# Gated attention and feed-forward decode: wq and the first four key units split between two issuing engines

## The chip, the core and the metric

The kernel runs on one core of a Trainium2 chip. The core has five engines with their own instruction streams: TensorE (PE, matrix products), VectorE (DVE), ScalarE (ACT), GpSimd (POOL) and SyncE (SP). SyncE and ScalarE can each issue transfers (DMAs); the data is moved by sixteen DMA engines that all issuers share. An instruction stream runs in program order, and an engine that waits for a semaphore holds up all that stands behind the waiting instruction, the issue of transfers too. The metric is the device time of one execution in microseconds (us), as a median over runs.

## The reference

One token (`x`, 512 numbers) goes through an attention block with a long cache and through a gated feed-forward block, and a sigmoid gate mixes the two:

```python
g = sigmoid((x * gate_w).sum(-1))
q = x @ wq                                  # 32 heads of 128, wq 512 x 4096 (8 MB)
scores = q . k_cache * 128 ** -0.5          # 8 key heads, each used by 4 query heads, 32768 keys of 128
a = softmax(scores) . v_cache @ wo          # wo 4096 x 512
b = (silu(x @ w1) * (x @ w3)) @ w2          # 1792 wide
out = g * a + (1 - g) * b
```

All of it is float32. Keys and values are 128 MiB each, read once; all that is read comes to 296.23 MB.

## The kernel before, in words

**Buffers and units.** Keys and values come in units of 8 MB: 128 partitions by 16384 numbers, so a row of 64 KB in each partition. Two buffers of that size, `big[0]` (called A) and `big[1]` (B), take everything that is streamed. Each buffer has a left and a right half of 32 KB a partition, `region(b, z)` with z = 0 or 1, and the program tracks them under the keys A0, A1, B0 and B1. There are sixteen key units (t = 0 to 15, two heads to four units) and sixteen value units, which run four units behind (`LAG = 4`). `wq` goes to A first. Key units 0 and 2 go to B, units 1 and 3 to A (`where(t)`); from unit 4 on keys go to A and values to B.

**The order of the work.** Nothing is scheduled automatically. `Program` (L24) records each instruction in the order in which `add` is called, works out from the tiles read and written which semaphores it must wait for, and then each engine's list is emitted as it stands. A transfer is one more instruction in the list of the engine that issues it. `load` (L190) records a transfer on SyncE; nine semaphores ("lanes") are used in turn. So the place of a `load` call among the other calls decides where it stands in SyncE's list, and the tiles that it overwrites decide what it waits for.

**The start.** SyncE issues `wq` (L203), then key unit 0 (`load_keys(0)`, L488), neither with a wait. ScalarE issues the small transfers of `x` and `gate_w` (L202, 2 KB each). TensorE turns `x` into columns (L253), VectorE copies them to `xp` (L259), and 64 products with `wq` follow (L268), which need both `xp` and all of `wq`. ScalarE then does the gate's activation (L280), copies the query out of the accumulators (L286), and after two transposes copies it in sixteen pieces to `win` (L296). `winc` (L324) is the window on `win` that TensorE uses as weights for the scores.

**One key unit.** For unit t, ScalarE copies three quarters of the right half to a spare tile (`set_aside`, L318), VectorE transposes the keys in eight steps of 32 columns (L346; four from the left half, one from the right half, three from the spare tile), and TensorE multiplies each step with `winc` (L330). VectorE's steps alternate between two tiles, so a step waits for the products of the step before the last. Afterwards ScalarE copies the scores out of the accumulator (`scores_out`, L358), and the next unit's transfer is recorded after these (L502), before `winc` of the next unit. Every fourth unit a softmax follows (`turn`, `softmax`). After unit 3 the feed-forward weights w1 and w3 are loaded into B (L454) and multiplied (L463); from then on each round also loads and uses a value unit (L413, L432). The tail (L529 to L690) finishes the last heads and streams wo and w2 in pieces.

Of the kernel before, what the change touches and what calls it, by code (L numbers as in the profile page):

```python
# [116 lines left out]
def kernel(  # L117
# [13 lines left out]
    nc = tc.nc  # L131
# [5 lines left out]
    NC = D // P  # L137
# [7 lines left out]
    R = NB * DH  # L145
    NP = HKV // 2
    NH = 4 * NP
    LAG = 4
# [12 lines left out]
    def sbuf(name, *shape):  # L161
        return nc.alloc_sbuf_tensor(name, [P, *shape], F32)[:]

    big = [sbuf("big_a", 2 * R), sbuf("big_b", 2 * R)]
# [20 lines left out]
    ps_s, ps_o, *pm = [nc.alloc_psum_tensor(f"ps{i}", [P, 512], F32)[:] for i in range(4)]  # L185


    lanes = [0]

    def load(dst, src, writes, over=()):  # L190
        lanes[0] += 1
        lane = f"load{lanes[0] % 9}"
        return pr.add(
            "SP", lambda: nc.sync.dma_start(dst, src), writes=writes, over=[*over, lane], inc=lane, by=16, also=lane,  # L194
        )

    def region(b, z):
        return big[b][:, z * R:(z + 1) * R]


    for i, t in enumerate((x.rearrange("a b n -> (a b) n"), gate_w.rearrange("(o n) -> o n", o=1))):
        pr.add("ACT", lambda i=i, t=t: nc.scalar.dma_start(rows[i][0:1, :], t), writes=[f"row{i}"], inc="row", by=16)  # L202
    load(big[0], wq.rearrange("(p c) n -> p (c n)", c=NC), ["A0", "A1"])  # L203


    ident, ones, fold = sbuf("ident", P), sbuf("ones", P), sbuf("fold", 32)
# [37 lines left out]
    def clear(**kw):  # L244
        pe(zeros,
           reads=["acc"], writes=["s"], **kw)
# [40 lines left out]
    for b in range(2):  # L287
        qt = kt[b][:, 0:512]
        dve(lambda b=b, qt=qt: V.transpose(qt, rows[b]), reads=[f"row{b}"], writes=[f"kt{b}"])
        for j in range(4):  # L290
            w, u = divmod(4 * b + j, 2)
            src = qt[32 * j:32 * j + 32, :].rearrange("p (q c x) -> p x c q", q=4, c=4)[:, 0]
            for e in range(2):
                r, o = 2 * u + e, 16 + 8 * e + 4 * u
                dst = win[32 * r:32 * r + 32, w, :, o:o + 4]
# [5 lines left out]
    kd = k_cache.rearrange("a (w u) s d -> w (a u s d)", u=2).rearrange("w (p m r) -> w m p r", p=P, m=4)  # L301
    vd = v_cache.rearrange("a h (e p n) d -> (a h) e p (n d)", e=2, p=P)

    def where(t):
        return 1 if t in (0, 2) else 0

    def load_keys(t):
        b = where(t)
        load(big[b], kd[t // 4, t % 4], ["AB"[b] + str(z) for z in range(2)])
# [6 lines left out]
    def set_aside(t):  # L316
        src, key = region(where(t), 1).rearrange("p (n r) -> p n r", n=NB), "AB"[where(t)] + "1"
        act(lambda: A.copy(spare, src[:, :, 32:128]), reads=[key], writes=["wo"])  # L318
        if t == LAG - 1:
            act(lambda: A.copy(extra, src[:, :, 0:32]), reads=[key], writes=["extra"], over=["B1"])  # L320

    def window(t, z):
        return act(
            lambda: A.copy(winc, win[:, t // 4, :, 16 - 16 * z:48 - 16 * z]),  # L324
            reads=[("win", t // 4, r) for r in range(4)], writes=["winc"], credit="windows",
        )
# [9 lines left out]
    def scores(t, z, win_op):  # L336
        kin = region(where(t), z).rearrange("p (n c j) -> p c n j", c=4, j=32)
        ks = []
        for c in range(4):
            src, key = kin[:, c], "AB"[where(t)] + str(z)  # L340
            if (z, c) >= (1, 1):
                src, key = spare[:, :, 32 * (c - 1):32 * (c - 1) + 32], "wo"
            elif z == 1 and t == LAG - 1:
                src, key = extra, "extra"
            dst = kt[c % 2].rearrange("p (n i) -> p n i", i=32)
            k = dve(lambda d=dst, s=src: V.transpose(d, s), reads=[key], writes=[f"kt{c % 2}"], credit="keys")  # L346
            pe(lambda c=c: scores_part(c), reads=[f"kt{c % 2}", "winc"], writes=["s"], loop=True,
               credits=((win_op, 1), (k, 1)) if c == 0 else ((k, 1),))
            ks.append(k)

        if t == LAG - 1 and z == 0:
            done = dve(lambda: V.tensor_copy(mark2, ones[:, 0:1]), reads=["ones"], writes=["mark2"])
            for k in ks:
                k.via = done

    def scores_out(t):
        o = act(
            lambda: A.copy(sb[:, :, :, t % 4], ps_s.rearrange("p (n i) -> p n i", i=32)),  # L358
            reads=["s"], writes=[("sb", t % 4)], credit="scores",
        )  # L360
        return o
# [9 lines left out]
    def turn(loop, credits=()):  # L371
        for f in range(4):
            pe(lambda f=f: turn_part(f), reads=[("sb", m) for m in range(4)] + ["ident"], writes=[f"f{f}"], loop=loop,
               credits=credits if f == 0 else ())
# [29 lines left out]
    def total(w):  # L404
        dve(lambda: V.tensor_reduce(  # L405
            sums[:, 8 * w:8 * w + 8].rearrange("p (u q) -> p u q", u=2),
            probs[:, :, 0:1024].rearrange("p u (n q) -> p u q n", q=4), axis=AX.X, op=ALU.add,
        ), reads=[("prob", u) for u in range(2)], writes=[("sums", w)])


    def load_values(s):
        return pr.add(
            "SP", lambda: nc.sync.dma_start(big[1], vd[s // 2, s % 2]), writes=["B0", "B1"], over=["extra"],  # L413
            credit="values", by=16,
        )

    def weights(s):
        u, e = s // 2 % 2, s % 2
        return act(
            lambda: A.copy(  # L420
                pv[:, 0:512].rearrange("p (y r) -> p y r", r=64),
                prob[u][:, 0:1024].rearrange("p (y e r) -> p y e r", e=2, r=64)[:, :, e],
            ), reads=["pvpad", ("prob", u)], writes=["pv"], over=["o"], credit="weights",
        )
# [13 lines left out]
    def values_loop(vt, wt, credits):  # L438
        pe(values_all, reads=["B0", "B1", "pv", "pvpad"], writes=["o"], credits=(*credits, (vt, 16), (wt, 1)), loop=True)


    def own(s):
        h, e = divmod(s, 2)
        dve(lambda: V.tensor_tensor(
            tmp[:, e], ps_o.rearrange("p (b d) -> p b d", b=4), own_b.unsqueeze(2).to_broadcast([P, 4, P]), op=ALU.mult,
        ), reads=["o", "own_b"], writes=[f"tmp{e}"])
        if e == 1:
            dve(lambda: V.tensor_reduce(red[h], tmp.rearrange("p e b d -> p d (e b)"), axis=AX.X, op=ALU.add),  # L448
                reads=["tmp0", "tmp1"], writes=[("red", h)])


    def load_hidden():
        for z, t in enumerate((w1, w3)):
            load(big[1][:, z * NC * F:(z + 1) * NC * F], t.rearrange("(p c) f -> p (c f)", c=NC), [f"B{z}"])  # L454

    def hidden_products():
        for z in range(2):
            def ff(z=z):
                t = big[1][:, z * NC * F:(z + 1) * NC * F]
                for c in range(NC):  # L460
                    for j in range(4):
                        o = c * F + FJ * j
                        ins = T.matmul(  # L463
                            pm[z][32 * j:32 * j + 32, 0:FJ], xp[:, c, :], t[:, o:o + FJ],
                            start=(c == 0), stop=(c == NC - 1),
                        )
                return ins
            pe(ff, reads=[f"B{z}", "xp"], writes=[f"m{z}"])
# [16 lines left out]
        pr.add(e, lambda: q.dma_start(outs[2 * i:2 * i + 2, :], src[31 + 64 * i:33 + 64 * i, :]),  # L485
               reads=[key], writes=[("out", i)], inc=inc, by=16)

    load_keys(0)  # L488
    vals = {}
    first = window(0, 0)  # L490
    for t in range(NH):
        v = t - LAG
        set_aside(t)
        scores(t, 0, first)
        scores(t, 1, window(t, 1))
        out_op = ((scores_out(t), 1),)
        if v < 0:
            clear(loop=True, credits=out_op)
        if t == LAG - 1:
            load_hidden()  # L500
        if t + 1 < NH:
            load_keys(t + 1)  # L502
            first = window(t + 1, 0)
        if v >= 1:
            own(v - 1)
        if t % 4 == 3:
            turn(v >= 0, out_op if v >= 0 else ())
        if v >= 0:
            values_loop(vals.pop(v), weights(v), () if t % 4 == 3 else out_op)
            clear(loop=True)  # L510
        if t == LAG - 1:
            hidden_products()
        if v + 1 >= 0 and t + 1 < NH:
            vals[v + 1] = load_values(v + 1)

        if t % 4 == 3:
            softmax(t // 4)
        if t % 4 == 0 and t > 0:
            total(t // 4 - 1)
        if t == LAG:  # L520
            hidden()
# [175 lines left out]
    a, b, c, d = flips  # L697
# [67 lines left out]
```

## Time and profile before

| | |
|---|---|
| median of 3 runs | 694.2 us (694.1 to 694.31) |
| profiled execution | 693.89 us, of which the span of instructions is 692.1 us |
| moved by DMA | 296.35 MB, mean 428 GB/s |
| busy | PE 388.3 us (56%), DVE 370.1 (53%), ACT 134.7 (19%), POOL 2.8 |

In rows of the profile an instruction stands as line, engine, operation, what it writes and reads, and its shape; "x8" is a count. In the listing by time the first two numbers are start and duration in us from the start of the span, and the brackets say how long the engine was idle before and what ended that. "SPq" and "ACTq" are the parts of SyncE and ScalarE that issue transfers; the duration of such a row is that of the issue, not of the movement, and when a transfer has landed is seen at the instruction that waited for it. The engines' busy shares are averages over the whole span.

### The profile page before, as it was taken

To read this page: it belongs to the slowest core of one execution; us is meant where nothing else is said; L and a number is where in the kernel's file an instruction comes from. 1 tells how busy PE (TensorE), PEld (TensorE's weight loads), DVE (VectorE), ACT (ScalarE), POOL (GpSimd) and SP (SyncE) were. 2 spreads that over 40 slices of the span, in tenths; PEclk is the share of its full clock that TensorE was granted. 3 is DMA by queue.
4 is the path that set the end of the run, shared out by engine and by line. 5 is a ranking of instruction groups with operands and counts; after the bars stand their busy time and mean duration, and the time that the engine had idled before them with its cause. 6 is when DMAs were issued, how large, how long until landed. Compare 5 with 4: busy or idle time off the path is not lost. (4 is left out here: it accounts for less than half of the span.)

```text
span 692.1 us, 5789 instructions
## 1 busy us (share of the span) xinstructions
PE 388.3 (56%) x2448; PEld 95.3 (14%) x2448; DVE 370.1 (53%) x259; ACT 134.7 (19%) x113; POOL 2.8 (0%) x15
## 2 busy tenths in 40 slices
PE   1537677566473636565564646364563646564457
PEld 0101111201010101201010101101010101211112
DVE  1049998493725637493826537492816547600701
ACT  0143323222303131220303131220303031100000
POOL 1000000000000000000000000000000000000000
PEclk9969999968686966778695779788697879865789
DMA  9999999999999999999999999999999999999996
GB/s 394 444 432 424 428 424 432 449 439 432 424 432 424 443 447 432 428 428 428 432 443 443 428 428 428 428 443 447 432 424 428 428 436 439 421 451 425 422 429 287
DMA packets 6213, 296.35 MB, mean 428 GB/s; under 512 B 694, under 2 KB 698, under 8 KB 1084
## 3 DMA queue, kind: packets, MB, share of 16 engines
q1 hardware_dynamic: 6196, 296.23, 99.1%
q8 instruction: 6, 0.10, 0.1%
q14 instruction: 3, 0.02, 0.0%
q10 hardware_dynamic: 8, 0.01, 0.0%
HBM read 296.23 MB, written 0.00 MB: 428 GB/s over the span
## 5 line engine op out<-in xcount | busy, mean ns | idle before, releaser
L346 DVE STREAM_TRANSPOSE aside<-big_a 128x2048 f32<-128x2048 f32 x41 | 94.4, 2302 | 184.3 <-DMA big_a<-in_A_k_cache_dram 184.3
L330 PE MATMUL ps<-aside,winc 128*32 128x512 f32 x512 | 89.4, 776 | 168.0 <-PEq L703 167.2
L330 PE MATMUL ps<-kt,winc 128*32 128x512 f32 x512 | 89.0, 772 | 49.1 <-PEq L703 49.1
L318 ACT COPY aside<-big_a 128x6144 f32<-128x6144 f32 x14 | 74.4, 5313 | 171.2 <-DMA big_a<-in_A_k_cache_dram 171.2
L432 PE MATMUL ps<-big_b,pv 128*32 128x512 f32 x768 | 94.9, 650 | 17.4 <-PEq L703 17.4
L346 DVE STREAM_TRANSPOSE kt<-aside 128x2048 f32<-128x2048 f32 x32 | 72.7, 2273 | 0.0
L346 DVE STREAM_TRANSPOSE kt<-big_a 128x2048 f32<-128x2048 f32 x28 | 63.5, 2269 | 0.0
L330 PEld LDWEIGHTS ps<-aside,winc 128*32 128x32 f32 x512 | 13.1, 120 | 236.6 <-issue 236.6
L358 ACT COPY sb<-ps 128x512 f32<-128x512 f32 x16 | 17.1, 1071 | 136.5 <-PE ps L330 136.5
L432 PEld LDWEIGHTS ps<-big_b,pv 128*32 128x32 f32 x768 | 27.7, 119 | 85.0 <-issue 85.0
L346 DVE STREAM_TRANSPOSE aside<-aside 128x2048 f32<-128x2048 f32 x16 | 36.3, 2269 | 0.0
L587 PE MATMUL ps<-big_b,probs 128*32 128x512 f32 x128 | 19.1, 756 | 21.1 <-DMA big_b<-in_A_v_cache_dram 21.1
L330 PEld LDWEIGHTS ps<-kt,winc 128*32 128x32 f32 x512 | 13.1, 120 | 125.4 <-issue 125.4
L596 DVE TENSOR_SCALAR red<-ps,own_b 128x128 f32<-128x128 f32 x2 | 0.7, 350 | 52.7 <-PE ps L587 52.7
L324 ACT COPY winc<-win 128x128 f32<-128x128 f32 x32 | 9.8, 307 | 77.9 <-PE ps L330 77.9
L587 PE MATMUL ps<-big_a,probs 128*32 128x512 f32 x128 | 18.1, 730 | 7.6 <-DMA big_a<-in_A_v_cache_dram 7.6
L346 DVE STREAM_TRANSPOSE aside<-big_b 128x2048 f32<-128x2048 f32 x7 | 16.0, 2291 | 11.0 <-DMA big_b<-in_A_k_cache_dram 11.0
L641 PE MATMUL ps<-win,ones 128*128 128x512 f32 (+1 forms) x40 | 21.8, 631 | 0.0
L242 PE MATMUL ps<-acc 128*128 128x512 f32 x34 | 20.0, 670 | 2.5 <-POOL acc L213 1.5
L379 DVE TENSOR_REDUCE mt<-turned 128x8 f32<-128x2048 f32 x4 | 9.2, 2292 | 20.3 <-PE turned L368 20.3
L405 DVE TENSOR_REDUCE sums<-probs 128x8 f32<-128x2048 f32 x4 | 15.3, 3834 | 2.1 <-ACT probs L398 2.1
L268 PE MATMUL turned<-big_a,xp 128*32 128x512 f32 x64 | 8.6, 699 | 12.0 <-DMA big_a<-in_A_wq_dram 12.0
(94 smaller groups left out, 186.9 us busy)
## 6 DMA issues: line engine op xcount, KB each, us to landing
big_b<-in_A_v_cache_dram SPq DMA_DIRECT2D x2, 4096.0 KB, 25.8
big_b<-in_B_w_dram SPq DMA_DIRECT2D x2, 3584.0 KB, 20.8
aside<-in_A_wo_dram SPq DMA_DIRECT2D x1, 4096.0 KB, 29.4
big_a<-in_A_wo_dram SPq DMA_DIRECT2D x1, 4096.0 KB, 20.4
big_a<-in_B_w_dram SPq DMA_DIRECT2D x2, 1024.0 KB, 23.5
big_a<-in_B_w_dram SPq DMA_DIRECT2D x1, 768.0 KB, 26.0
big_a<-in_B_w_dram SPq DMA_DIRECT2D x1, 512.0 KB, 26.7
big_a<-in_B_w_dram SPq DMA_DIRECT2D x1, 256.0 KB, 26.9
```

The lines of the kernel that those rows point to most:

```text
L242: return T.matmul(ps_s, acc[:, 0:P], acc, start=True, stop=False, skip_group_check=True)
L268: ins = T.matmul(pf[b][32 * j:32 * j + 32, :], xp[:, c, :], t[:, o:o + REP * DH], start=(c == 0), stop=(c == NC - 1),)
L318: act(lambda: A.copy(spare, src[:, :, 32:128]), reads=[key], writes=["wo"])
L324: lambda: A.copy(winc, win[:, t // 4, :, 16 - 16 * z:48 - 16 * z]),
L330: ins = T.matmul(ps_s[32 * g:32 * g + 32, :], winc[:, c, :], kt[c % 2][:, 512 * g:512 * g + 512], start=False, stop=False, skip_group_chec ...
L346: k = dve(lambda d=dst, s=src: V.transpose(d, s), reads=[key], writes=[f"kt{c % 2}"], credit="keys")
L358: lambda: A.copy(sb[:, :, :, t % 4], ps_s.rearrange("p (n i) -> p n i", i=32)),
L379: dve(lambda: V.tensor_reduce(mt[:, 0:8], turned.rearrange("p (n q) -> p q n", q=8), axis=AX.X, op=ALU.max), reads=banks, writes=["mt"])
L405: dve(lambda: V.tensor_reduce(sums[:, 8 * w:8 * w + 8].rearrange("p (u q) -> p u q", u=2), probs[:, :, 0:1024].rearrange("p u (n q) -> p u ...
L432: ins = T.matmul(ps_o[32 * t:32 * t + 32, :], pv[:, o:o + 32], big[1][:, n * P:(n + 4) * P], start=((z, g) == (0, 0)), stop=((z, g) == (1, ...
L587: ins = T.matmul(ps_o[32 * t:32 * t + 32, :], prob[u][:, o:o + 32], vt[:, n * P:(n + 4) * P], start=((e, z, g) == (0, 0, 0)), stop=((e, z, ...
L641: return T.matmul(bank[:, 0:n], ones, win.rearrange("p w c n -> p (w c n)")[:, 0:n], start=True, stop=True)
```

## The change

`wq` and the key units 0 to 3 no longer come as one transfer each. Each comes as two, with rows of 32 KB over all partitions: the left half is issued by SyncE and the right half by ScalarE, each with nine semaphores of its own. The two halves of `wq` are recorded ahead of `x` and `gate_w`. The halves of unit 0 are recorded where `load_keys(0)` stood. For units 1 to 3 the right half of unit t + 1 is recorded at the top of round t, ahead of `set_aside(t)`, and the left half where the whole unit stood. From unit 4 on nothing is changed.

In ScalarE's list the right half of `wq` thus stands first, ahead of `x` and `gate_w`; the right half of unit 0 stands after the copies to `win` (L296) and ahead of the first `winc` copy; the right half of unit 1 stands behind that copy; those of units 2 and 3 stand behind the copy of the scores and the `winc` copy of the round before and ahead of that round's `set_aside`. In SyncE's list the left halves stand where the whole units stood.

```diff
-    lanes = [0]
+    lanes = {"SP": 0, "ACT": 0}
 
-    def load(dst, src, writes, over=()):
-        lanes[0] += 1
-        lane = f"load{lanes[0] % 9}"
+    def load(dst, src, writes, over=(), eng="SP"):
+        q = nc.sync if eng == "SP" else nc.scalar
+        lanes[eng] += 1
+        lane = f"{eng}{lanes[eng] % 9}"
         return pr.add(
-            "SP", lambda: nc.sync.dma_start(dst, src), writes=writes, over=[*over, lane], inc=lane, by=16, also=lane,
+            eng, lambda: q.dma_start(dst, src), writes=writes, over=[*over, lane], inc=lane, by=16, also=lane,
         )
+
+    def load_half(b, z, src):
+        load(region(b, z), src[:, z * R:(z + 1) * R], ["AB"[b] + str(z)], eng=("SP", "ACT")[z])
...
+    for z in range(2):
+        load_half(0, z, wq.rearrange("(p c) n -> p (c n)", c=NC))
     for i, t in enumerate((x.rearrange("a b n -> (a b) n"), gate_w.rearrange("(o n) -> o n", o=1))):
         pr.add("ACT", lambda i=i, t=t: nc.scalar.dma_start(rows[i][0:1, :], t), writes=[f"row{i}"], inc="row", by=16)
-    load(big[0], wq.rearrange("(p c) n -> p (c n)", c=NC), ["A0", "A1"])
...
-    load_keys(0)
+    for z in range(2):
+        load_half(where(0), z, kd[0, 0])
     vals = {}
     first = window(0, 0)
     for t in range(NH):
         v = t - LAG
+        if t + 1 < LAG:
+            load_half(where(t + 1), 1, kd[0, t + 1])
         set_aside(t)
         scores(t, 0, first)
         scores(t, 1, window(t, 1))
...
         if t + 1 < NH:
-            load_keys(t + 1)
+            if t + 1 < LAG:
+                load_half(where(t + 1), 0, kd[0, t + 1])
+            else:
+                load_keys(t + 1)
             first = window(t + 1, 0)
```

## The prediction

> **What bounds the kernel now.** I read the page's head, slices and queues first, then the DMA rate in windows, then the start in order of time.
>
> ```profile
> span 692.1 us, 5789 instructions
> DMA  9999999999999999999999999999999999999996
> q1 hardware_dynamic: 6196, 296.23, 99.1%
> L346 DVE STREAM_TRANSPOSE aside<-big_a 128x2048 f32<-128x2048 f32 x41 | 94.4, 2302 | 184.3 <-DMA big_a<-in_A_k_cache_dram 184.3
> ...
> 43.30:62.60 19.30, 13.83 (x71) 2.85 (x72) 17.73 (x8) 5.91 (x3) 0.00 (x0) 0.82 1.00 435
> 140.00:660.00 520.00, 290.72 (x1820) 69.08 (x1820) 282.89 (x190) 94.45 (x71) 0.00 (x0) 0.76 1.00 433
> ...
> 661.57 26.71 DMA big_a<-in_B_w_dram
> ```
>
> The sixteen DMA engines are busy in every slice, and SyncE's queue q1 carries 99.1% of that. In the windows the last two numbers are DMA share and GB/s: share 1.00 and 433 GB/s over 520 us in the middle. VectorE, with the key transposes (L346), waits 184.3 us for keys, and the chain ends in a transfer. So the kernel is a stream of 296.23 MB that hardly stops. Compute has slack behind it, so what counts is whether the change makes the stream stop: a microsecond with nothing queued can't be won back later, because there is no free rate to win it with.
>
> The start, in order of time (start, duration, what; in brackets the idle time and what ended it):
>
> ```profile
> 0.93 0.40 SPq L194 DMA_DIRECT2D big_a<-in_A_wq_dram  x1
> 0.96 0.53 ACTq L202 DMA_DIRECT2D probs<-in_A_x_dram  x1
> 1.39 0.41 SPq L194 DMA_DIRECT2D big_b<-in_A_k_cache_dram  x1
> 1.52 0.23 ACTq L202 DMA_DIRECT2D probs<-in_gate_w_dram  x1
> 10.38 0.61 PE L253 MATMUL ps<-ident,probs 1*128 1x1 f32 x4 [6.76 <-DMA probs<-in_gate_w_dram]
> 11.02 0.17 DVE L259 COPY xp<-ps 128x4 f32<-128x4 f32 x1 [7.15 <-PE ps L253]
> 23.01 8.62 PE L268 MATMUL turned<-big_a,xp 128*32 128x512 f32 x64 [12.02 <-DMA big_a<-in_A_wq_dram]
> 31.69 0.33 SPq L194 DMA_DIRECT2D big_a<-in_A_k_cache_dram  x1
> 35.31 1.88 ACT L296 COPY win<-kt 32x16 f32<-32x16 f32 x8
> 37.22 0.30 ACT L324 COPY winc<-win 128x128 f32<-128x128 f32 x1
> 43.30 2.31 DVE L346 STREAM_TRANSPOSE aside<-big_b 128x2048 f32<-128x2048 f32 x1 [9.34 <-DMA big_b<-in_A_k_cache_dram]
> ...
> 62.65 2.31 DVE L346 STREAM_TRANSPOSE aside<-big_a 128x2048 f32<-128x2048 f32 x1 [1.62 <-DMA big_a<-in_A_k_cache_dram]
> ...
> 0.00:2.00 2.00, 0.46 (x1) 0.46 (x2) 0.00 (x0) 0.22 (x1) 1.02 (x7) 1.00 0.49 165
> ```
>
> wq has landed at 23.0, key unit 0 at 43.30 and unit 1 at 62.65. The last interval, 19.35 us, is the price of a full 8 MB transfer (window above: 435 GB/s), so a half costs 9.67 us, and one 64 KB row of the eight that each engine has costs 2.42, a 32 KB row 1.21. From an empty queue wq took 23.0 - 0.93 = 22.05, so an issue into an empty queue loses 2.70 us. Of this about 1.1 passes before the first row moves (165 GB/s x 2.00 us is 330 KB, five rows, begun before 2.00). Note what keeps the stream whole: unit 0 is issued at 1.39, behind wq and waiting for nothing, so unit 1 may come as late as 31.69.
>
> **The change part by part.** The kernel before runs on two buffers; unit 0 and 2 go to B, wq and units 1 and 3 to A. After, each of these five transfers is a left half issued by SyncE and a right half issued by ScalarE. ScalarE's program order decides the rest.
>
> Rows of half size: near free. Near the end two 4 MB halves with 32 KB rows land one after the other:
>
> ```profile
> 660.80 3.64 PE L587 MATMUL ps<-big_b,probs 128*32 128x512 f32 x32 [1.11 <-DMA big_b<-in_A_v_cache_dram]
> ...
> 670.51 5.70 PE L587 MATMUL ps<-big_b,probs 128*32 128x512 f32 x32 [6.07 <-DMA big_b<-in_A_v_cache_dram]
> ```
>
> 9.71 us against 9.67: 0.04 each, ten halves 0.4 at most. Both halves of wq share the engines, so wq is whole at 23.0 as before and the left half of unit 0, behind it on SyncE, at 23.0 + 9.67 = 32.65.
>
> First step: x and gate_w move behind the right half of wq on ScalarE's queue. Before, they had that queue to themselves, and gate_w still took 10.38 - 1.52 = 8.86 us, or 3.7 row times of 2.42, because SyncE's rows take turns with it. After, they get no turn until the right half of wq is through (about 23.0), and then take turns with 32 KB rows of unit 0: 3.7 x 1.21 = 4.5 us, so they land at 27.5. Bounds: 23.0 (no extra time) and 31.8 (8.86 again). I take 27.5 since rows are half as long. Then transposes, the copy to xp and the handover: 0.81 us from 10.38 to 11.19, with the wake-up 0.85. The products with wq (L268) start at 28.35 instead of 23.01, a delay d = 5.3 us (bounds 0 and 9.7). Their cover before was that xp was ready at 11.19, 12 us ahead of wq; that cover is gone. All that follows them moves by d: SyncE's issue for unit 1 (left), which waits for them, to 37.0; the copies into win to 42.5.
>
> The stream meanwhile: SyncE has only the left half of unit 0 left, which ends at 32.65, and ScalarE can't issue the right half of unit 0 until it has passed the gate's activation and sixteen copies (L296), at 37.19 + 5.3 = 42.5. Before, this transfer stood in the queue from 1.39. So the queues run dry: unit 1 (left) issued at 37.0 with 2.70 to start lands at 37.0 + 2.70 + 9.67, against 32.65 + 9.67 in an unbroken stream. **First stop: 37.0 + 2.70 - 32.65 = 7.0 us** (bounds 1.7 and 11.4 by d).
>
> Second step: the right half of unit 0 is late, and what it holds up. Rows for the chain behind it:
>
> ```profile
> 52.40 1.06 PE L330 MATMUL ps<-kt,winc 128*32 128x512 f32 x8 [0.36 <-PEq L703]
> ...
> 55.71 0.33 SPq L194 DMA_DIRECT2D big_b<-in_A_k_cache_dram  x1
> ...
> 58.76 2.27 DVE L346 STREAM_TRANSPOSE kt<-aside 128x2048 f32<-128x2048 f32 x1
> 61.17 1.06 PE L330 MATMUL ps<-kt,winc 128*32 128x512 f32 x8 [1.13 <-PEq L703]
> ...
> 63.17 0.32 ACT L324 COPY winc<-win 128x128 f32<-128x128 f32 x1
> 63.38 5.32 ACT L318 COPY aside<-big_a 128x6144 f32<-128x6144 f32 x1
> ```
>
> Right 0 is issued at 42.5 and gets turns from 43.6 (1.1 later), row about with left 1. Left 1 alone would be through at 49.05 (landing at 49.4 less some 0.35), so 5.45 us of it are left; shared, it ends at 54.5, with as much of right 0 done. By then left 2 is queued: its buffer half is free when the left scores of unit 0 are done, which need winc (37.22 + 0.30 + d, and 0.33 for the issue now before it, 43.2) and four steps at 2.2 us behind it as between 43.30 and 52.40, so it is issued about 51. It takes every second turn, so the remaining 4.2 us of right 0 take 8.4: it lands near 63.3, not 43.30.
>
> Then nothing of the old cover is left: the copy to the spare tile (5.32) lay under the left transposes before, now the last three transposes wait for it. 63.3 + 5.3 + 3 x 2.2 = 75.2; from the end of the last transpose (61.03 before) to the end of the winc copy (63.49) it is 2.46; so ScalarE issues right 2 at 77.7. It stands behind that copy in program order, where SyncE before issued unit 2 at 55.71. The queue has work until right 1 and left 2 are through: four halves from 37.0 + 2.70, that is 78.4. **Second stop: 77.7 + 2.70 - 78.4 = 2.0 us** (bounds 0, if right 0 gets more than every second turn, and 3.3 if it first moves 2.7 after its issue; shifting with d as a whole, it doesn't depend on it).
>
> Next late things: left 3 needs the left scores of unit 1 (75.2, four transposes of 2.2 and TensorE's last step, 61.03 to 62.23 above: 85) while right 2 runs to 90; unit 4, issued when unit 3's transposes are read, near 119, has the feed-forward weights ahead of it until 126; the first values follow the products with these weights:
>
> ```profile
> 116.80 2.27 DVE L346 STREAM_TRANSPOSE kt<-aside 128x2048 f32<-128x2048 f32 x1
> ...
> 124.32 6.22 PE L463 MATMUL ps<-big_b,xp 128*32 128x448 f32 x64
> ...
> 137.91 2.31 DVE L346 STREAM_TRANSPOSE aside<-big_a 128x2048 f32<-128x2048 f32 x1 [6.55 <-DMA big_a<-in_A_k_cache_dram]
> ```
>
> These end at 130.54, 11.5 after the last transposes of unit 3 (119.07); after, those end near 128, so values are issued at 139.6 against a stream that has work until about 145. So no third stop. ScalarE's five new issues (0.23 to 0.53 us each) lie in its waits; the one before winc costs 0.33 of a 2.5 us margin (51 + 1.1 against 54.5).
>
> A gain to set against: unit 0 took 43.30 - 23.0 = 20.3 us, 0.97 more than unit 1. If what slowed it falls into the first stop, up to 1.0 comes back; with the row cost of 0 to 0.4 I take -0.5. **Sum: 7.0 + 2.0 - 0.5 = 8.5 us.** The profiled execution took 693.89 us (span 692.1), 0.3 below the median of 694.2: 693.89 + 8.5 = 702.4.
>
> **The rivals.**
> *x and gate_w aren't held up* (d = 0): ScalarE's queue might let tiny transfers by. For it: they're 2 KB each. Against: they'd have to pass rows queued ahead on the same queue. First stop 31.69 + 2.70 - 32.65 = 1.7, second 2.0: 693.89 + 3.7 - 0.5 = 697.1.
> *No second stop*: right 0 is served faster than every second turn, or compute is quicker. 693.89 + 6.5 = 700.4.
> *Turns are whole runs of rows.* If an engine served one queue's eight rows in a go, x and gate_w would wait for all of left 0, to about 33: d = 10.8, first stop 31.69 + 10.8 + 2.70 - 32.65 = 12.5; right 0, issued at 48.0, would follow left 1 (54.9) in one go at 64.6, right 2 be issued at 79.0, in time for a queue that lasts to 83.9. 693.89 + 12.5 = 706.4. Against it: by this gate_w would before have come with wq at 23.0, and it released TensorE at 10.38. [...]
> *Faster: two queues carry more than one.* Place: 0 to 23 and 43 to 78, when both have work, some 58 us at today's rate. Price: each per cent saves 0.6 us, so it must pass 15% (about 500 GB/s) to beat 8.5; at 20% it gives 11.6 - 8.5, or 690.8. For it: no row shows two loaded queues, and wq's start is slow. Against: share 1.00 at 435 GB/s, so no engine has time left between rows. [...]
>
> **How the numbers follow.** Chances: the forecast 0.66, x and gate_w unheld 0.15, no second stop 0.08, whole runs 0.06, faster 0.05. The likeliest gives 702.4. Range: down to 697.0 for the unheld rival, up to 707.5, which is the upper bound of d (693.89 + 11.4 + 2.0 = 707.3) and the whole-runs case. Below lie the faster case and the low tail of the unheld one. Within 0.2% (1.4 us, what a measurement of this kernel can tell from no change) falls only that tail with no second stop and the 1.0 regained: 0.03. Slower 0.92.
>
> **What would show it.** In the changed kernel: L253's products start near 27.5 and L268's near 28.4, not 23.0; SyncE's third issue near 37, ScalarE's second issue for keys near 42; a stretch from about 32 to 38 with a DMA share near 0; the copy to the spare tile for unit 0 near 63 instead of 43.30; right 2 issued near 78 with a second, short hole; unit 4 landing near 146 instead of 137.91, and from there the same stream. I'm wrong if the first hole is missing, if x lands early, if the share in shared stretches goes past 435 GB/s, or if the end doesn't move by what unit 4 moved.

## The result and the profile after

The changed kernel takes 705.17 us (median of 4 runs, 704.81 to 705.64) against 694.15 for the kernel before; the ratio is 1.0159, with a 95% interval of 1.0142 to 1.0177. It is slower, as forecast (702.4, range 697.0 to 707.5), by 11.0 us where 8.5 were worked out. The profiled execution took 705.19 us, with a span of 703.4.

Lines of the page of the changed kernel (span; DMA share in 40 slices; the queues of SyncE, q1, and of ScalarE, q10):

```profile
span 703.4 us, 5795 instructions
...
DMA  9779999999999999999999999999999999999996
...
q1 hardware_dynamic: 6196, 275.25, 90.8%
q10 hardware_dynamic: 728, 20.98, 7.0%
```

Two slices near the start have dropped from 9 to 7; the rest is as before. Windows of the changed kernel (last two numbers: DMA share, GB/s):

```profile
32.00:39.00 7.00, 6.42 (x50) 1.65 (x42) 0.15 (x1) 0.54 (x3) 0.00 (x0) 1.00 0.01 2
39.00:62.00 23.00, 7.65 (x36) 1.40 (x36) 10.26 (x6) 4.32 (x19) 0.00 (x0) 0.76 1.02 433
...
78.00:82.00 4.00, 3.73 (x23) 0.88 (x20) 3.82 (x3) 3.83 (x3) 0.00 (x0) 1.00 0.76 270
...
82.00:92.00 10.00, 7.30 (x45) 1.64 (x38) 10.00 (x5) 2.99 (x2) 0.00 (x0) 1.00 1.02 413
92.00:102.00 10.00, 8.10 (x44) 1.77 (x46) 9.72 (x6) 5.98 (x3) 0.00 (x0) 1.00 0.95 403
...
146.00:670.00 524.00, 285.00 (x1816) 69.18 (x1820) 285.13 (x190) 97.30 (x72) 0.00 (x0) 0.77 1.00 433
```

The DMA engines stand still from 32 to 39 us, dip again after 78, and stay somewhat low until 102 (413 and 403 GB/s). From 39 to 62 and from 146 on they run at the 433 GB/s of before. The start of the changed kernel, in order of time:

```profile
27.41 0.61 PE L258 MATMUL ps<-ident,probs 1*128 1x1 f32 x4 [23.79 <-DMA probs<-in_gate_w_dram]
...
28.27 9.84 PE L273 MATMUL turned<-big_a,xp 128*32 128x512 f32 x64 [0.26 <-DVE xp L264]
...
38.18 0.33 SPq L195 DMA_DIRECT2D big_a<-in_A_k_cache_dram  x1
...
64.50 5.31 ACT L323 COPY aside<-big_b 128x6144 f32<-128x6144 f32 x1 [20.51 <-DMA big_b<-in_A_k_cache_dram]
...
78.08 0.33 ACTq L195 DMA_DIRECT2D big_b<-in_A_k_cache_dram  x1
...
87.24 0.33 SPq L195 DMA_DIRECT2D big_a<-in_A_k_cache_dram  x1
...
149.15 2.31 DVE L351 STREAM_TRANSPOSE aside<-big_a 128x2048 f32<-128x2048 f32 x1 [5.68 <-DMA big_a<-in_A_k_cache_dram]
...
187.84 5.31 ACT L323 COPY aside<-big_a 128x6144 f32<-128x6144 f32 x1 [15.24 <-DMA big_a<-in_A_k_cache_dram]
```

x and gate_w release TensorE at 27.41 instead of 10.38, the left half of unit 1 is issued at 38.18 instead of 31.69, the right half of unit 0 lands at 64.50, and unit 4 lands at 149.15 instead of 137.91. That is 11.2 us later, and the execution is 11.3 longer (705.19 - 693.89): the whole loss is made before unit 4, and none of it comes back.

### The profile page after: what moved, and what is told of

It reads as the page before. It is cut to its first block, busy times and chain, and to the rows that moved or that the text cites. A ratio compares the mean times of both kernels' runs of the same rounds, so it can differ in the third digit from the quotient of the medians.

```text
span 703.4 us, 5795 instructions
## 1 busy us (share of the span) xinstructions
PE 385.8 (55%) x2448; PEld 95.4 (14%) x2448; DVE 370.8 (53%) x259; ACT 134.7 (19%) x113; POOL 2.8 (0%) x15
## 3 DMA queue, kind: packets, MB, share of 16 engines
q1 hardware_dynamic: 6196, 275.25, 90.8%
HBM read 296.23 MB, written 0.00 MB: 421 GB/s over the span
## 5 line engine op out<-in xcount | busy, mean ns | idle before, releaser
L437 PE MATMUL ps<-big_b,pv 128*32 128x512 f32 x768 | 90.9, 628 | 17.6 <-PEq L714 17.6
L323 ACT COPY aside<-big_b 128x6144 f32<-128x6144 f32 x2 | 10.6, 5316 | 20.5 <-DMA big_b<-in_A_k_cache_dram 20.5
## 6 DMA issues: line engine op xcount, KB each, us to landing
big_b<-in_A_k_cache_dram SPq DMA_DIRECT2D x2, 4096.0 KB, 27.4
big_a<-in_A_k_cache_dram ACTq DMA_DIRECT2D x2, 4096.0 KB, 27.5
big_a<-in_A_wq_dram SPq DMA_DIRECT2D x1, 4096.0 KB, 21.8
```

The source lines that it names most:

```text
L437: ins = T.matmul(ps_o[32 * t:32 * t + 32, :], pv[:, o:o + 32], big[1][:, n * P:(n + 4) * P], start=((z, g) == (0, 0)), stop=((z, g) == (1, ...
```

## The experiments

My theory: the time grows by as long as the stream stands still. A stop is the issue of the first half of unit 1 (SyncE), plus 2.70 us to start, less the time at which what was queued before is through: 32.65 while the right half of unit 0 isn't queued, 42.3 when all of it is (32.65 and another half, 9.67; the expectations below were worked out with 42.65, which is 0.3 too much by these terms). Rival A: two queues or 32 KB rows are slower in themselves. Rival B: the late x alone is the loss.

To compare the rest, I take the landing of unit 4 less its landing in a stream unbroken after that issue. After left 1 is issued, seven halves (67.7 us), the feed-forward weights (16.9, as their two transfers of 3584 KB are seven eighths of a unit) and unit 4 (19.35) are to come while right 0 is late: 2.70 + 103.9 in all. For the changed kernel this is 149.15 - (38.18 + 106.6) = 4.4 us. With unit 0 out of the way, 94.3 us are to come instead of 103.9.

**x and gate_w ahead of the right half of wq.**

```diff
-    for z in range(2):
-        load_half(0, z, wq.rearrange("(p c) n -> p (c n)", c=NC))
     for i, t in enumerate((x..., gate_w...)):
         pr.add("ACT", ...)
+    for z in range(2):
+        load_half(0, z, wq.rearrange("(p c) n -> p (c n)", c=NC))
```

> The changed kernel with x and gate_w issued by ScalarE ahead of the right half of wq; all else as changed. My theory (the stream stops because the late x moves the left half of unit 1 while the right half of unit 0 is not queued yet): the products with wq start at 23.0 again, the first stop shrinks from 8.2 to about 1.7 us, the second (1.4) and the rest (1.7) stay: 699 us, between 698 and 700. Rival A (two queues or 32 KB rows are slower in themselves): no change, 705. Rival B (the late x alone is the loss): all of it goes, 695.

Measured 704.23 us (703.7 to 704.77), ratio 1.0142 (1.0125 to 1.0159). My number was wrong by 5 us. Its timeline:

```profile
8.28 0.61 PE L258 MATMUL ps<-ident,probs 1*128 1x1 f32 x4 [4.66 <-DMA probs<-in_gate_w_dram]
...
27.65 9.70 PE L273 MATMUL turned<-big_a,xp 128*32 128x512 f32 x64 [18.77 <-DMA big_a<-in_A_wq_dram]
...
37.41 0.33 SPq L195 DMA_DIRECT2D big_a<-in_A_k_cache_dram  x1
```

x is early now (8.28), but wq isn't: the products wait for it until 27.65, and left 1 is issued at 37.41, as late as before. The right half of wq is now the third transfer in ScalarE's list, issued at 1.78, and the left half of unit 0, issued at 1.37, is ahead of it in time and shares the engines with it. So the edit moved the lateness from x to wq, and doesn't separate the theories (the nearest number was rival A's 705, which the next experiments rule out): the stop by my rule is 37.41 + 2.70 - 32.65 = 7.5, against 8.2. Whoever holds up the products, the stop follows.

**Both halves of unit 0 early, x late as in the change.** The lines below stand right behind those for x and gate_w, with `kd` and `where` moved up.

```diff
+    for z in range(2):
+        load_half(where(0), z, kd[0, 0])
...
-    for z in range(2):
-        load_half(where(0), z, kd[0, 0])
```

> The changed kernel with both halves of unit 0 recorded right behind x and gate_w, so that ScalarE issues the right half of unit 0 at about 2 us and not at 42.5; x stays behind the right half of wq. My theory: the products with wq still start near 28, unit 1 (left) is still issued near 38, but unit 0 fills the stream until 42.6, so the first stop is gone; the right half of unit 0 lands near 43, so the second is gone too: 694.2 to 696. Rival A (two queues or 32 KB rows are slower in themselves): 703 to 705. Rival B (the late x alone is the loss): 702 or more, since x is as late as before.

Measured 694.61 us (694.52 to 695.76), ratio 1.0010 (1.0000 to 1.0019):

```profile
37.12 0.33 SPq L195 DMA_DIRECT2D big_a<-in_A_k_cache_dram  x1
```

Left 1 is issued at 37.12, after products as late as in the changed kernel, and yet the loss is gone but for some 0.5 us. Rivals A and B both fall here: 21 MB still go over ScalarE's queue, and x is still late.

**Both edits together.** x and gate_w first, and unit 0 early.

> Both edits: x and gate_w first, then the right half of wq, then the right half of unit 0; the halves still go over two queues. My theory: no stop is left, 694.2 to 695.5, the same as with unit 0 early alone. Rival A (two queues or 32 KB rows are slower in themselves): 703 to 705. Rival B: 695.

Measured 694.45 us (694.11 to 694.82), ratio 1.0002 (0.9993 to 1.0012). The share in the window in which the changed kernel stood still is whole again, while ScalarE's queue moves the same bytes:

```profile
32.00:39.00 7.00, 4.47 (x42) 1.37 (x34) 1.46 (x3) 2.11 (x8) 0.00 (x0) 1.00 0.96 414
```

So two queues neither cost nor gain anything that these runs can tell.

**Only wq split.** Key units whole on SyncE as before (`load_keys(0)` and `load_keys(t + 1)` restored).

> Only wq comes as two halves over two queues, ahead of x and gate_w; all key units whole on SyncE as in the kernel before. My theory: x is as late as in the changed kernel (products with wq start near 28, unit 1 issued near 38), but unit 0 stands whole in SyncE's queue until 42.6, so no stop: 694.0 to 694.8. Rival A: a few tenths of that, since only wq uses two queues: 694 to 695. Rival B (the late x alone is the loss): 700 or more.

Measured 697.04 us (696.42 to 697.37), ratio 1.0036 (1.0022 to 1.0050), so 2.9 us over the 694.13 of the same chip, against my 0 to 0.7. The timeline shows why:

```profile
32.58 0.61 PE L258 MATMUL ps<-ident,probs 1*128 1x1 f32 x4 [28.97 <-DMA probs<-in_gate_w_dram]
...
43.43 0.33 SPq L195 DMA_DIRECT2D big_a<-in_A_k_cache_dram  x1
...
65.57 2.31 DVE L351 STREAM_TRANSPOSE aside<-big_a 128x2048 f32<-128x2048 f32 x1 [0.73 <-DMA big_a<-in_A_k_cache_dram]
...
141.42 2.31 DVE L351 STREAM_TRANSPOSE aside<-big_a 128x2048 f32<-128x2048 f32 x1 [7.15 <-DMA big_a<-in_A_k_cache_dram]
```

x came at 32.58 and not at 27.4. After wq's end, taken as the 23.0 of the changed kernel (0.96 + 22.0 from issue to landing), it took 9.6 us beside rows of 64 KB, and in the changed kernel 4.4 us beside rows of 32 KB: the lateness goes with the row size, as it would if the tiny transfers take turns with whole rows. I had used the changed kernel's time without seeing that. By the rule for the stop, 43.43 + 2.70 - 42.3 = 3.8 us, against 2.9 measured (unit 4 lands 3.5 later than before, 141.42 against 137.91): the rule came within a microsecond where my input to it was wrong.

**Only the keys split.** wq whole on SyncE, x and gate_w alone on ScalarE at the start; the key halves at the places of the change.

```diff
-    for z in range(2):
-        load_half(0, z, wq.rearrange("(p c) n -> p (c n)", c=NC))
+    load(big[0], wq.rearrange("(p c) n -> p (c n)", c=NC), ["A0", "A1"])
```

> wq whole on SyncE and x and gate_w alone ahead on ScalarE's queue, as in the kernel before; only the four key units come as halves, at the places of the changed kernel. My theory (the stop is the issue of unit 1's left half, plus 2.70 us, less the end of unit 0's left half at 32.65): the products with wq start at 23.0, unit 1 (left) is issued at 31.7, the first stop is 1.75 us and not 8.2, the later losses (about 3) stay: 699 us, 698 to 700. Rival (the late right half of unit 0 costs its whole delay, whenever unit 1 is issued): 704 to 705.

Measured 699.22 us (697.68 to 701.48), ratio 1.0066 (1.0050 to 1.0081):

```profile
23.07 9.81 PE L272 MATMUL turned<-big_a,xp 128*32 128x512 f32 x64 [12.13 <-DMA big_a<-in_A_wq_dram]
...
32.94 0.33 SPq L195 DMA_DIRECT2D big_a<-in_A_k_cache_dram  x1
...
143.71 2.31 DVE L350 STREAM_TRANSPOSE aside<-big_a 128x2048 f32<-128x2048 f32 x1 [5.50 <-DMA big_a<-in_A_k_cache_dram]
```

As expected. The right half of unit 0 is as late as in the change, but left 1 is issued at 32.94; the stop by the rule falls from 8.2 to 3.0, and the time by 6.0. What is lost after that issue stays: 143.71 - (32.94 + 106.6) = 4.2 us, against 4.4. The four runs spread from 697.68 to 701.48, and the profiled one is the slowest of them: unit 4 lands 5.8 us late in it, and it loses another 1.8 later on that this account doesn't explain.

**x behind both right halves, unit 0 early.**

> The changed kernel with both halves of unit 0 early and x and gate_w behind both right halves on ScalarE's queue, so x is much later than in the changed kernel while unit 0 is early. My theory: x lands near 43 when unit 0 is through, the products start near 44 and take 9.8 us, unit 1 (left) is issued near 53.7; stop = 53.7 + 2.70 - 42.65 = 13.8 us: 707.9, between 706.5 and 709.5. Rival (x isn't what holds the stream, only the late right half of unit 0 is): 694 to 696.

Measured 707.18 us (706.64 to 708.26), ratio 1.0193 (1.0177 to 1.0209), 13.0 us over before:

```profile
42.65 0.61 PE L264 MATMUL ps<-ident,probs 1*128 1x1 f32 x4 [39.03 <-DMA probs<-in_gate_w_dram]
...
52.29 0.33 SPq L195 DMA_DIRECT2D big_a<-in_A_k_cache_dram  x1
...
150.61 2.31 DVE L353 STREAM_TRANSPOSE aside<-big_a 128x2048 f32<-128x2048 f32 x1 [3.95 <-DMA big_a<-in_A_k_cache_dram]
```

The stop by the rule is 52.29 + 2.70 - 42.3 = 12.7 us. A late x costs next to nothing while unit 0 covers it (0.5 us, with left 1 issued at 37.12, in the experiment with unit 0 early), and by the rule it costs in full once left 1 is issued after about 40 us.

**All halves on SyncE**, in the order of the kernel before.

> The same ten halves with 32 KB rows, but all issued by SyncE in the order of the kernel before; x and gate_w alone on ScalarE's queue. My theory: no stop, row size costs 0 to 0.4 us: 694.0 to 694.8; if the left half of unit 1 being issued before the right changes anything it is below that. Rival (rows of half the size are what costs): 697 or more.

Measured 694.38 us (694.28 to 695.18), ratio 1.0004 (0.9995 to 1.0014). Its page counts 6916 packets on q1 against 6196 before, for the same 296.23 MB, at no cost that shows. Row size is no cause.

**TensorE kept busy before x.** `clear()` is called 20 times, then 26 times instead of once.

> The changed kernel with nineteen more clearing products on TensorE ahead of the transposes of x, so that TensorE is busy until about 26 us; the result is unchanged. It tests the 1.2 us by which the products with wq are longer in the changed kernel (9.84 against 8.62 us). If that is TensorE starting slow after long idleness, they now take some 7 to 8.6 us, unit 1 (left) is issued 1.2 to 2.8 us earlier and the time falls by as much: 702.4 to 704.0. If the slow products are no term of the sum: 705.2 as before.

With twenty, 703.85 us (703.38 to 706.04), ratio 1.0153 (1.0137 to 1.0169). Its added products ended at 21.25, six microseconds before x, and the products with wq took 9.51 us, so it didn't do what it was for. The time fell by 1.3 all the same and lies in the range expected, but not for the reason given: left 1 was issued at 38.09, as late as before. What fell is the loss after that issue, 147.16 - (38.09 + 106.6) = 2.5 us instead of 4.4. Its five runs lie in two groups (three below 703.9, two above 706), and I can't say why.

> The changed kernel with twenty-five more clearing products on TensorE, so that it is busy until about 27 us, right up to the transposes of x (with nineteen they ended at 21.25, and the products with wq took 9.51 us all the same). If the slow first products come of the idle time before them, they now take 7 to 8 us, unit 1 (left) is issued 1.8 to 2.8 us earlier than at 38.18, and the time falls by as much against 705.2: 702.4 to 703.4. If they stay slow: above 703.8.

With twenty-six, 703.13 us (702.02 to 703.67), ratio 1.0127 (1.0112 to 1.0143):

```profile
28.60 7.07 PE L274 MATMUL turned<-big_a,xp 128*32 128x512 f32 x64 [0.26 <-DVE xp L265]
...
35.73 0.33 SPq L195 DMA_DIRECT2D big_a<-in_A_k_cache_dram  x1
```

The added products now end at 26.5. The same 64 products take 7.07 us and left 1 is issued 2.45 us earlier. The time fell by 2.0, within the range expected. So the first products after idleness were slow here: 9.84 us in the changed kernel, where TensorE was idle for 23.8 us before x's transposes, 9.51 after 6.4 us with twenty, and 7.07 after 1.2 us with twenty-six. This is a term of the first stop. How much of it the end shows is less sure, as the kernel with twenty gained 1.3 with its issue at 38.09.

**Right halves of units 2 and 3 on SyncE**, behind the left ones and no longer behind the copy of the scores in ScalarE's list; once on the changed kernel, once on the one with only the keys split.

```diff
-        if t + 1 < LAG:
+        if t == 0:
             load_half(where(t + 1), 1, kd[0, t + 1])
...
                 load_half(where(t + 1), 0, kd[0, t + 1])
+                if t > 0:
+                    load_half(where(t + 1), 1, kd[0, t + 1], eng="SP")
```

> The changed kernel, but the right halves of units 2 and 3 are issued by SyncE right behind the left ones, so they no longer stand behind the copy of the scores in ScalarE's list; those of wq and units 0 and 1 stay on ScalarE. My theory (the second stop, and a smaller one at unit 3, come from that place in ScalarE's list): the right half of unit 2 is issued near 72.5 and not at 78.1, the queue doesn't run dry near 79, the first stop stays: 705.2 less 1.4 to 2.2, so 703.0 to 703.8. Rival (the rest of the loss lies elsewhere, in the unevenness of the DMA engines after the first stop): 705.2.

> The same edit on top of the kernel with only the keys split (wq whole, x early; 699.2 us): the right halves of units 2 and 3 issued by SyncE. My theory: only the first stop of about 2 to 3 us is left: 696.5 to 698. Rival: 699.2 as with them on ScalarE.

Measured 704.23 us (703.6 to 704.6), ratio 1.0148 (1.0133 to 1.0164), and 698.99 us (697.3 to 699.66), ratio 1.0065 (1.0051 to 1.0079): 0.9 and 0.2 us better than without the edit, less than I expected of either. The first of them, in order of time:

```profile
36.97 0.33 SPq L195 DMA_DIRECT2D big_a<-in_A_k_cache_dram  x1
...
142.06 0.33 SPq L418 DMA_DIRECT2D big_b<-in_A_v_cache_dram  x1
...
145.84 2.31 DVE L351 STREAM_TRANSPOSE aside<-big_a 128x2048 f32<-128x2048 f32 x1 [3.02 <-DMA big_a<-in_A_k_cache_dram]
...
185.91 5.31 ACT L323 COPY aside<-big_a 128x6144 f32<-128x6144 f32 x1 [17.54 <-DMA big_a<-in_A_k_cache_dram]
```

The second stop did go: unit 4 lands at 145.84, and 145.84 - (36.97 + 106.6) = 2.3 us is lost after the issue, against 4.4. (That left 1 comes 1.2 us earlier here than in the changed kernel isn't the edit's doing: the products with wq took 8.41 us in this execution.) But a new wait took its place. The first value unit is issued at 142.06, when unit 4 is nearly through; unit 5 follows unit 4 by 40.07 us (185.91 - 145.84), against 38.69 in the changed kernel (187.84 - 149.15). So 1.4 of the 2.1 us are given back. The kernel with the keys only shows the same:

```profile
32.60 0.33 SPq L195 DMA_DIRECT2D big_a<-in_A_k_cache_dram  x1
...
141.35 2.31 DVE L350 STREAM_TRANSPOSE aside<-big_a 128x2048 f32<-128x2048 f32 x1 [3.10 <-DMA big_a<-in_A_k_cache_dram]
...
181.01 5.31 ACT L322 COPY aside<-big_a 128x6144 f32<-128x6144 f32 x1 [17.14 <-DMA big_a<-in_A_k_cache_dram]
```

141.35 - (32.60 + 106.6) = 2.2 us lost after the issue instead of 4.2, and 39.66 us from unit 4 to unit 5. After late scores the values are the next thing to be late.

The stops by the rule and the measured loss against before on the same chip:

| kernel | first half of unit 1 issued | stop by the rule, us | measured loss, us |
|---|---|---|---|
| changed | 38.18 | 8.2 | 11.0 |
| x ahead | 37.41 | 7.5 | 10.1 |
| right halves 2 and 3 on SyncE | 36.97 | 7.0 | 10.2 |
| TensorE busy, 20 | 38.09 | 8.1 | 9.7 |
| TensorE busy, 26 | 35.73 | 5.8 | 9.1 |
| only keys split | 32.94 | 3.0 | 5.0 |
| only keys, right halves 2 and 3 on SyncE | 32.60 | 2.7 | 5.0 |
| unit 0 early, x last | 52.29 | 12.7 | 13.0 |
| only wq split | 43.43 | 3.8 | 2.9 |
| unit 0 early | 37.12 | none | 0.5 |
| unit 0 early, x ahead | 36.22 | none | 0.3 |

In the seven rows with a late right half of unit 0 the loss is the stop plus 1.5 to 3.3; in the four without, the stop less 0.9 to plus 0.5. The stops are read from the profiled execution and the losses from medians; the two are furthest apart for the kernel with only the keys split (701.48 profiled, 699.22 median).

## Why the prediction was right

**x and gate_w late: right.** Forecast to land at 27.5, they released TensorE at 27.41; the products were to start at 28.35 and started at 28.27. The argument by turns (3.7 row times of half the length) is borne out by the kernel with only wq split, where rows of twice the size give 9.6 us instead of 4.4. The rivals of x unheld and of turns in whole runs of rows fall with that row.

**The first stop: right in kind, too small.** Forecast 7.0 us, with left 1 issued at 37.0; it was issued at 38.18, and the stop by the rule is 8.2. The term that was mis-sized is the length of the products, taken as 8.62 us from before and measured as 9.84. Weight loads of the changed kernel's products, from 28.27 on, show it (start, duration, four at a time):

```profile
32.54 0.20 PEld L273 LDWEIGHTS turned<-big_a,xp 128*32 128x32 f32 x4 [0.66 <-issue]
33.39 0.20 PEld L273 LDWEIGHTS turned<-big_a,xp 128*32 128x32 f32 x4 [0.66 <-issue]
34.08 0.12 PEld L273 LDWEIGHTS turned<-big_a,xp 128*32 128x32 f32 x4 [0.48 <-issue]
34.51 0.12 PEld L273 LDWEIGHTS turned<-big_a,xp 128*32 128x32 f32 x4 [0.31 <-issue]
```

A group takes 0.85 us until 33.39 and 0.43 from 34.08, while the granted clock reads 1.00 in the window from 32 to 39. Before the change, x's transposes at 10.38 were as far from the products as in the kernel with only the keys split, which took 9.81, so the length isn't set by the change: it lies between 8.4 and 9.9 in these executions (8.41 and 9.84 in two that start alike), and 7.07 when TensorE had been busy until just before. The slow part lasts 5.8 us here (28.27 to 34.08), 5.9 in the kernel with only wq split (33.44 to 39.32) and 3.3 in the one with unit 0 early (28.44 to 31.72); what sets its length isn't shown by these runs.

**The second stop: right in place, its issue partly by luck.** Forecast: right 0 lands at 63.3, right 2 is issued at 77.7. Measured 64.50 and 78.08. By the forecast's own rule the measured issues give 78.08 + 2.70 - 79.6 = 1.2 us, not 2.0 (79.6 is 38.18 + 2.70 and four halves); the window from 78 to 82, at 270 GB/s, lacks 1.5 us of work at 433. The forecast let ScalarE's issues wait until the copies ahead of them had ended. Here they didn't:

```profile
42.52 0.35 ACTq L195 DMA_DIRECT2D big_b<-in_A_k_cache_dram  x1
...
42.99 0.69 ACT L301 COPY win<-kt 32x16 f32<-32x16 f32 x3
...
78.08 1.09 ACT L363 COPY sb<-ps 128x512 f32<-128x512 f32 x1 [8.06 <-PE ps L335]
78.08 0.33 ACTq L195 DMA_DIRECT2D big_b<-in_A_k_cache_dram  x1
78.95 0.32 ACT L329 COPY winc<-win 128x128 f32<-128x128 f32 x1
```

Right 0 is issued at 42.52 while copies to `win` that stand ahead of it run until 43.68, and right 2 at 78.08, just as the copy of the scores starts and before the `winc` copy. The forecast so put each of these issues about 1.2 us too late for what stood ahead of it (43.68 against 42.52; and from the end of the last transpose, at 76.81, to the issue of right 2 it had 2.46 us where 1.27 were measured). This made up for products and transposes that came later than forecast.

**What is lost behind the first stop: too small.** The forecast's 2.0 us stood for all of it. By the landing of unit 4 it is 4.4, and the kernel before has 1.3 by the same count (137.91 less 0.93 + 2.70 + 133.0 for its five 8 MB transfers, the weights and unit 4), so 3.1 more. With 8.2 that makes the 11.3 us by which the profiled execution is longer. The forecast saw "no third stop", with left 3 issued near 85 and work queued until 90. Left 3 was issued at 87.24, and by the rule this is still in time, though barely: 87.24 + 2.70 = 89.9, with work until 78.08 + 2.70 + 9.67 = 90.45. Yet from 82 to 102 the stream lacks about 1.2 us of work at 433 GB/s (413 and 403 in the windows above; the kernel before moves 433 in that stretch). So the denial of a third loss is the part of the mechanism that failed; what slows the stream there was not tested, and the rest of the 4.4 isn't assigned either. The two kernels with right halves 2 and 3 on SyncE show that 2.0 to 2.1 of the 4.4 hang on their place in ScalarE's list.

**The gain of up to 1.0 set against it: not seen in the sum.** The 8.2 and 3.1 us make up the whole loss without it. With only wq split, unit 1 lands 2.9 us later than before (65.57 against 62.65) where the stop by the rule is 3.8, so 0.9 seems to come back there, and 0.6 is lost again before unit 4. In the changed kernel the landings in between can't be read in this way, so whether the gain is hidden in the 3.1 stays open.

**Two queues carry more than one: wrong, as held.** In the shared stretch from 39 to 62 the changed kernel moves 433 GB/s (442 from 43 on, which the kernel before reaches too, from 39 to 62 on one queue), and with both edits, no stop and the two queues in use the time is that of before (1.0002).

**That the stream has no slack: right.** Unit 4 lands 11.2 us later, and the end comes 11.3 later.

## What to carry to other kernels

In a kernel that lives on one full stream, ask of an edit what is queued at each moment and which instruction issues the next transfer: a transfer that needs no wait belongs in a list where nothing that waits stands ahead of it (694.61 us with unit 0 early, 705.17 without). A transfer moved to a compute engine's queue inherits that engine's program order: here the right half of unit 0, which waits for nothing, was issued at 42.52, and the whole unit before at 1.39. A small transfer put behind a large one on its queue came only after the large one was through: x and gate_w released TensorE at 27.41, with wq whole at 23.0, and at 10.38 before. When one late issue is mended, look at once for the next one: here 1.4 of the 2.1 us won at the second stop were paid back at the first value unit.

## What the runs showed that I had not expected

A small transfer's delay went with the row size of the transfers beside it: 4.4 us after wq's end with 32 KB rows, 9.6 with 64 KB.

A half that was issued 0.85 us after its sister (1.78 and 0.93, with x and gate_w ahead of it on its queue) landed far more than that later: in the kernel with both edits, the halves of wq took 19.4 and 25.5 us from issue to landing, against 21.8 and 22.0 in the changed kernel, and wq was whole at 27.35 instead of 23.0 (at 27.65 in the kernel with x ahead alone). The unit queued behind the first half may have taken turns in the meantime; which rule of the queues decides that was not tested.

The 64 products with wq took 7.07 us when TensorE had been busy until 1.2 us before x came, and 8.4 to 9.9 us for the same work after idleness.
